# A fused attention, Fourier mixing and feed-forward kernel on one core: another order of all steps, and fifteen dummy matmul steps instead of sixteen

## The chip, the core and the metric

The kernel runs on one core of a Trainium2 chip. The core has a matrix engine (PE, whose weight loads are listed as PEld), a vector engine (DVE), a scalar engine (ACT), a general engine (POOL), a sync engine that only issues transfers here (SP), and sixteen DMA engines. Each engine works through its own instruction stream in order. The metric is the device time of one execution in microseconds (us), less is better. Times below come from four unprofiled runs and from one profiled execution.

## What is computed

Eight batches, eight heads, 576 rows, 64 columns a head. First a linear attention with exponential features, then a real two-dimensional Fourier transform added to the result, a normalisation, and a feed-forward block:

```python
proj = x @ w_phi;  proj -= max(abs(proj))
phi(x) = concat[exp(proj), exp(-proj)]            # 256 features
kv = phi(k)^T v;   z = sum(phi(k))
attn = (phi(q) kv) / (phi(q) z + 1e-6)            # per head, 576 x 64
x = attn with heads side by side                  # 576 x 512
u = x + real(fft(fft(x, axis=1), axis=2))
un = (u - mean(u)) / sqrt(var(u) + 1e-6)
out = u + relu(un @ w_ch1) @ w_ch2                # 512 -> 2048 -> 512
```

## The kernel before, in words

Nothing schedules this kernel at run time. The work of the eight batches is cut into some 1,240 steps, each a stretch of Python between two `yield`s that issues a few instructions on several engines. The string `PLAN` (from line 23) has one letter for each step, and the loop at the end issues the steps in that order (`step`, called over `PLAN`). So the order of the letters is the order of the instructions in every engine's stream, and in the transfer queues of POOL and SP as well. An instruction still waits for its operands and for a free buffer; while it waits, all that stands behind it on its engine waits too.

A letter names a stream, and the n-th use of a letter is the stream's n-th step. In the texts, "T1.0" is step 0 of stream T for batch 1.

- G and J (batch 0 only): transposes of keys and queries on PE (`turn_part`, L368), copied out by ACT (L373) or DVE (L375). J0.2 is the tile of the last 64 rows of the queries.
- T (`steps`): projections of keys (L477, L491; batch 0 L790, L804) and queries (L597; batch 0 L665, L697) on PE with the exponentials on ACT. T1.0 is `keys4` of batch 1, whose exponentials are L482 and L483.
- P (`maxima`): query projections whose absolute maximum DVE takes (L555; batch 0 L755, L772 in `widest4`, and `turn_m` L730 to L740). R (`kmax`): the same for keys (L511; batch 0 L838). S (`scaled`): POOL scales the values (L451, L466; batch 0 L852, L869).
- M (`mixing`): eight steps of key-value products (L887), the combination of the heads (L987, then L994 to L1002; six steps in batch 0, eight later), then the transform along the rows. For batches 1 to 7 that is M.16 (the matmul `pm`, L1021, and L1025 on DVE), M.17 (`again(1)`, L1034), M.18 (`along_rows`, L1045, with SS), M.19 (L1065 and `again(0)`), M.20 (L1045 with CS, and `px`) and M.21 to M.25 (`pu`, L1104). In batch 0 the same steps are M0.14 to M0.18 and on. D (`folded`): four DVE steps of sums and differences, L903 to L927; batch 0 copies a row on ACT in between (L916, L917).
- N and U: normalisation, its transpose (DMA, or PE in batch 0, L1159) and its scales. F (`forward`): 68 steps a batch of feed-forward: 32 of `hidden` (L1219 on PE, L1223 on ACT) and the rest of `output` (L1230 and L1277 on PE, L1236 on DVE).
- K, V, Q: loads of keys, values and queries of a later batch, issued by POOL (L284). B and A: their DMA transposes, issued by SP (L408, L410; L420 to L422). W: the loads of the two feed-forward weights (L93, L95), 2 MB each, by POOL. C, H, Z: constants, sines (L238 to L249, H0.0 to H0.3 are on ACT) and padding.
- Y (`stir`, L1325 to L1333): the dummy steps. Each issues four matmuls of 512 columns on a tile of ones into a PSUM tile that nobody reads (L1330). They use the PSUM pool `pk`, which has one buffer.

PSUM tiles come from three pools: `pj` (two buffers), `pk` (one) and `pb` (three). The order was written by a search outside the kernel; neither its costs nor its due times are in the file.

Of the kernel before, what the change touches and what calls it, by code (L numbers as in the profile page):

```python
# [20 lines left out]


PLAN = (
    "YYCCYCYGCGZTGRTGZTZTZRZJQQGSTJRKTPYTSTPRYTWJJJRMPTMTSSMTPPSTPTMTZQMTMMTMPMMVKBTCMTMDTYMVHMYYDYYDDAHM"
    "HYYHTHMMMHKMTTRMNMTMYQNNYVMSNTKNMFFNFNRRFSTPFTPTUFWMNFFMNFFSFRTFVMFFTCURPSYUBNTUTFSUFMFQKTFMFTPPMQTP"
    "VMTFFPUTFUMTMFFAFMMTFFMQFMFDFRFMFTVFFFFRFMFTFFMFFPFFTFFFQDDFFFRFMFTKFFDMTFFFFTFMFFMFRTFMRTFMFSSSSTTM"
    "NPFFTNPBTMMMSMQFTMTPPMFFMFFTMFFFPVTAMFFFPNFFMTFFMNNKUMFFVMMFFQTMFFTFRMRFFTFFFQFMFFMFMFFFPTFFRFFFFDFD"
    "VFTPFFFDFFDKTPRFTFFMMTSFFBFFFMMSSFFMFFRTMTMFFTNMSMFFFTNPPMFMTFFFTMTFSTPMFFFMFFQPFTFMFFVFNMFFFMKTFFAM"
    "NNMFFMFUMFVFFMVQFFMFTTRFFMFFFKFRFFMTQFFFDTMRFFFFFDTPFFFTDDFRPFFFFFMTFTFMFFMFBMRFSSMFFTTTMFMTFFFTFNFN"
    "SFMTTMMFFFPMFTMSTPPMFFSMTFFMNFPFMFFPFFVKMNQKFFMNMUFFMFFMFFVMFAFMFQMFFMFTTRFQRFFFTVFMFFFFDFTPFRFFFPDT"  # L30
    "FFFTFFFDFFFDRTMTMFFFFMBFSMFFSMRFTFTTMSFMFTFNMMMTMFTFFFMNFPSSTMTNFFFFTPPMFFFMFTFPQMFVFKFPFFMFFMANMFFN"
    "FFMKFFMFTUTFMFFRFRFFSVFMFFFFFTMFTFQFRMFDVTFFFMTRFFDFFFFFFFDFFDFTMFTBQFMFFMSFMFRFMFTFTTMFFSMTNFTNFFMP"
    "SMFFMMTFMPTFSMTFFMTPFMFTFFQMFNPPPFVMFFAMFFPFNNUMVFMFTFMFMFFFMFRFFMTRTFSFFFFFPFFMFVFMTFFRFFTFDFDFPTFF"
    "FFDDFRFFTTMMFFFFFFMMFRSFTFFMTFTMTFFNTFSMNFFFMTFTTFMFMFMTSPFMFFFFMFFSMFTPPMFFFMFFMNPFMFFPNNFUMMFFFFMF"
    "FMFFFMMFFFFFFMFFMFFFDFFDFFFDFFDFMFFFFMMFMFMFFFMNMFNFFFFFFFFMMFFFFFFFFFFFFFFFFFFFFNMNFNFFFFFUFFFFFFFF"
    "FFFFFFFFFFFFFFFFFFFFFFFFFFFFFFFFFFFFFFF"
)


# [1 line left out]
def kernel(  # L41
# [11 lines left out]
    B, H, S, D = q.shape  # L53
    DF = w_phi.shape[1]
    C = H * D
# [1268 lines left out]
        return run  # L1324

    def stir(b):
        for i in range(16):
            ps = pk.tile([128, 512], F32, tag="pk", name="idle")
            for x in range(4):
                nc.tensor.matmul(  # L1330
                    ps[:], lhsT=ones_b[:], rhs=ones_b[:].unsqueeze(1).to_broadcast([128, 4, 128]),
                    start=True, stop=True,
                )  # L1333
            yield

    def fold_later(b):
# [4 lines left out]
        "U": (scales, 1), "P": (part(0), 7), "T": (part(1), 18), "R": (part(2), 5),  # L1341
        "S": (part(3), 5), "K": (fetch_k, 2), "V": (fetch_v, 3), "Q": (fetch_q, 3),
        "A": (arrive, 1), "B": (arrive_k, 1), "W": (load_ffn_weights, 2),
        "C": (constants, 6), "H": (sines, 6), "Y": (stir, 16), "G": (turn_first_k, 5), "J": (turn_first_q, 5), "Z": (pads, 6),
    }
    LONGER = {("N", 0): 10, ("U", 0): 7, ("M", 0): 24, ("T", 0): 20}
    at_ = {name: (1 if name in "KVBQA" else 0, 0) for name in STREAMS}
# [51 lines left out]
```

## Time and profile before

| | us |
|---|---|
| median of 4 runs (lowest, highest) | 429.33 (427.49, 430.65) |
| the profiled execution's own time | 428.03 |
| its span, first to last instruction | 426.3 |
| PE busy | 403.3 |
| DVE busy | 331.0 |
| ACT busy | 311.6 |
| POOL busy | 207.7 |
| dummy matmuls, 64 of L1330, busy | 19.1 |
| feed-forward matmuls L1219, L1230, L1277, busy | 141.7, 125.0, 14.9 |

The span is shorter than the time by 1.7 us, which lies before the first and after the last instruction. Busy matmuls overlap (one is started before the last has drained), so the sum of single durations is more than busy time. The granted PE clock is 1.00 in nearly the whole run; its mean is 0.994.

### The profile page before, as it was taken

The numbers are of one execution on the slowest core, as the hardware profiler recorded it, in microseconds if no ns is written. First come the engines' busy times: TensorE is split into PE (matmuls) and PEld (weight loads), VectorE is DVE, ScalarE is ACT, GpSimd is POOL, SyncE is SP. The second block draws the span as 40 slices with busy tenths as digits, with TensorE's granted clock in tenths as the row PEclk, the third lists the DMA queues.
The fourth block names the chain that finished last, engine by engine and source line by source line (L and its number), as shares of the span: only waits on it lengthen the run. The fifth ranks groups of instructions, "written<-read, shape, count | busy, mean of one in ns | idle before, by whom it ended". The sixth has DMA issues, their size and how long they took to land.

```text
span 426.3 us, 10494 instructions
## 1 busy us (share of the span) xinstructions
PE 403.3 (95%) x4126; PEld 255.6 (60%) x4126; DVE 331.0 (78%) x682; ACT 311.6 (73%) x690; POOL 207.7 (49%) x271
## 2 busy tenths in 40 slices
PE   8789789997999999999999999999999999999994
PEld 3465466643766558554775558565866567657562
DVE  5889787899789985998879885998899868965302
ACT  7986999747975799488947998688958796455450
POOL 7992578532964291826573273935554333300100
PEclk9899999999999999999999999999999999999999
DMA  8999879994698946994499269695472141104204
GB/s 219 176 185 162 116 91 168 146 139 86 116 133 85 115 80 93 120 110 84 83 160 121 52 80 132 85 115 104 78 97 49 27 87 32 27 1 79 68 23 86
DMA packets 108700, 42.70 MB, mean 100 GB/s; under 512 B 82859, under 2 KB 103595, under 8 KB 108651
## 3 DMA queue, kind: packets, MB, share of 16 engines
q0 software_dynamic: 45936, 16.60, 37.3%
q1 hardware_dynamic: 62479, 25.31, 33.7%
q8 instruction: 32, 0.52, 0.5%
q10 hardware_dynamic: 236, 0.13, 0.1%
q14 instruction: 17, 0.14, 0.1%
HBM read 36.77 MB, written 9.44 MB: 108 GB/s over the span
## 4 chain that ended last, share of the span: by engine, by line
PE 46%; DVE 32%; ACT 15%; issue 2%; POOL 2%; DMA 1%; DVEq 0%; ACTq 0%; POOLq 0%
PE psf L1219 16%; PE pso L1230 13%; DVE cb L999 5%; DVE R L903 4%; DVE MK L511 4%; DVE tg L994 4%; PE kv L887 3%; ACT HT L1223 2%; PE pso L1277 2%; DVE CEO L1034 2%; DVE MQ L555 2%; PE pu L1104 2%; DVE rd L1001 2%; DVE X L1236 2%; PE psD L1045 2%
## 5 line engine op out<-in xcount | busy, mean ns | idle before, releaser
L1219 PE MATMUL psf<-UT,W1b 128*128 128x320 bf16 (+1 forms) x1024 | 141.7, 286 | 1.5 <-ACT HT L1223 0.7
L1223 ACT ACTIVATE HT<-psf 128x256 bf16<-128x256 f32 (+1 forms) x256 | 100.8, 425 | 34.0 <-PE psf L1219 26.4
L1230 PE MATMUL pso<-W2b,HT 128*128 128x512 bf16 x512 | 125.0, 379 | 0.0
L1219 PEld LDWEIGHTS <-W1b 128*128 128x128 bf16 x1024 | 94.4, 98 | 29.8 <-issue 3.6
L1230 PEld LDWEIGHTS <-HT 128*128 128x128 bf16 x512 | 46.0, 98 | 44.8 <-issue 1.4
L1002 POOL TENSOR_TENSOR X<-cb,rd 128x320 f32<-128x320 f32 x56 | 41.5, 745 | 39.0 <-DVE rd L1001 36.1
L466 POOL TENSOR_TENSOR VCn<-VS,VCn 128x512 bf16<-128x512 bf16 x28 | 29.7, 1059 | 41.9 <-ACT VCn L461 33.5
L555 DVE TENSOR_REDUCE MQ<-psq 128x8 f32<-128x1024 f32 (+1 forms) x32 | 34.2, 1085 | 15.0 <-PE psq L547 14.7
L1236 DVE SCALAR_TENSOR_TENSOR X<-pso,rs,X 128x512 f32<-128x512 f32 x32 | 23.6, 736 | 22.0 <-PE pso L1230 21.9
L497 ACT ACTIVATE KPn<-psk 128x1024 bf16<-128x1024 f32 x28 | 28.6, 1020 | 14.7 <-DVE MK L511 14.5
L497 ACT ACTIVATE KPp<-psk 128x1024 bf16<-128x1024 f32 x28 | 28.8, 1027 | 11.1 <-PE psk L491 11.1
L451 POOL TENSOR_TENSOR V4N<-VS,V4N 64x256 bf16<-64x256 bf16 x14 | 8.8, 632 | 52.5 <-ACT V4N L447 47.7
L1094 DVE TENSOR_TENSOR X<-pu,X 128x512 f32<-128x512 f32 (+3 forms) x49 | 23.5, 529 | 14.0 <-PE pu L1104 13.8
L511 DVE TENSOR_REDUCE MK<-psk 128x8 f32<-128x1024 f32 x28 | 33.7, 1207 | 0.4 <-ACT KPn L497 0.3
L1190 POOL TENSOR_TENSOR rs<-VE,mhalf 128x5 f32<-128x5 f32 (+1 forms) x9 | 10.3, 1145 | 41.3 <-DVE VE L1189 41.2
L466 POOL TENSOR_TENSOR VCp<-VS,VCp 128x512 bf16<-128x512 bf16 x28 | 29.6, 1059 | 0.0
L606 ACT ACTIVATE QPHP<-psh 128x1024 bf16<-128x1024 f32 x28 | 29.1, 1039 | 0.5 <-PE psh L597 0.3
L606 ACT ACTIVATE QPHN<-psh 128x1024 bf16<-128x1024 f32 x28 | 29.3, 1045 | 0.0
L1150 ACT ACTIVATE UN<-X,MV 128x512 bf16<-128x512 f32 (+1 forms) x35 | 24.8, 724 | 5.4 <-issue 2.7
L1174 DVE BATCH_NORM_STATS2 st<-X 128x6 f32<-128x512 f32 (+1 forms) x40 | 27.0, 675 | 0.1
L284 POOL DMA_DIRECT2D QS<-in_q_dram x28 | 23.7, 849 | 4.0 <-DMA QT<-QS 4.0
L987 PEld LDWEIGHTS <-QPHP 128*128 128x128 bf16 x280 | 21.0, 98 | 4.5 <-DVE cb L999 0.5
(464 smaller groups left out, 800.6 us busy)
## 6 DMA issues: line engine op xcount, KB each, us to landing
out_dram<-X SPq DMA_DIRECT2D x16, 256.0 KB
out_dram<-X SPq DMA_DIRECT2D x64, 64.0 KB
QS<-in_q_dram POOLq DMA_DIRECT2D x14, 256.0 KB, 5.6
KS<-in_k_dram POOLq DMA_DIRECT2D x7, 512.0 KB, 6.9
VS<-in_v_dram POOLq DMA_DIRECT2D x14, 256.0 KB, 5.3
W1b<-in_moe_w_ch_dram POOLq DMA_DIRECT2D x1, 2048.0 KB, 13.9
W2b<-in_moe_w_ch_dram POOLq DMA_DIRECT2D x1, 2048.0 KB, 18.3
W2b<-in_k_dram SPq DMA_DIRECT2D x2, 512.0 KB
```

The lines of the kernel that those rows point to most:

```text
L466: nc.gpsimd.tensor_tensor(out=VC[:, hs, :, 0:D], in0=values[b][0][:, hs, :].rearrange("p h (j d) -> p h j d", d=D), in1=VC[:, hs, :, D:D + ...
L497: nc.scalar.activation(out=KP[:, hs, :, :].rearrange("p e (jp jj) f -> p jj (e jp) f", jj=2), in_=psk[:], func=AT.Exp, scale=sgn,)
L511: nc.vector.tensor_reduce(out=MK[:, 2 * pr:2 * pr + 2, :].rearrange("p e (jp jj) -> p jj (e jp)", jj=2), in_=tiles[pr][:], axis=AX.X, op=A ...
L555: nc.vector.tensor_reduce(out=o, in_=i[:], axis=AX.X, op=ALU.max, apply_absolute_value=True)
L606: nc.scalar.activation(out=o, in_=psh[:], func=AT.Exp, scale=sgn)
L1002: nc.gpsimd.tensor_tensor(out=X[:, :, D * h:D * h + D], in0=cb[:, :, 0:D], in1=rd[:].to_broadcast([128, 5, D]), op=ALU.mult,)
L1150: nc.scalar.activation(out=UN[0:M, c, :], in_=X[0:M, c, 0:C], func=AT.Identity, scale=-1.0, bias=mv[0:M, c, 0:1],)
L1174: nc.vector.bn_stats(out=st[0:M, :], in_=X[0:M, c, 0:C])
L1219: nc.tensor.matmul(ps[:], lhsT=W1b[:, cc, 128 * hh:128 * hh + 128], rhs=UT[:, cc, lo:hi], start=(cc == 0), stop=(cc == NCC - 1),)
L1223: nc.scalar.activation(out=HT[:, hh, lo:hi], in_=ps[:], func=AT.Relu, scale=-1.0)
L1230: nc.tensor.matmul(po[:], lhsT=HT[:, hh, at:at + 128], rhs=W2b[:, hh, :], start=(hh == 0), stop=(hh == NHH - 1),)
L1236: nc.vector.scalar_tensor_tensor(out=U[:, c, 0:C], in0=po[:], scalar=scale_of[b, c], in1=U[:, c, 0:C], op0=ALU.mult, op1=ALU.add,)
```

## The change

`PLAN` is replaced by another order of the same steps, and the dummy stream Y has 15 steps where it had 16. No other line differs: every other step is in both orders, once each.

```diff
 PLAN = (
-    "YYCCYCYGCGZTGRTGZTZTZRZJQQGSTJRKTPYTSTPRYTWJJJRMPTMTSSMTPPSTPTMTZQMTMMTMPMMVKBTCMTMDTYMVHMYYDYYDDAHM"
-    "HYYHTHMMMHKMTTRMNMTMYQNNYVMSNTKNMFFNFNRRFSTPFTPTUFWMNFFMNFFSFRTFVMFFTCURPSYUBNTUTFSUFMFQKTFMFTPPMQTP"
...
+    "YCYYCCYZZGCZGTTZGRZWGTTRTJGSTJRPTPSTYRTJRJPSTTMJMSSMPPZTTPMKQTMVMTMTMPMKMTTCQMMTBDQTHHYMMVKYAHHHHYYD"
+    "DYDMYTMMMMKTTVRMNWTMMYNTSNMNYNRRFFFNFSNUMTPTYPTFMFRTUFBFMSTFFFURCMUNSFNPMTTPPFSMQNUTFVMFFTFKMTQQTPM"
...
 )
...
     def stir(b):
-        for i in range(16):
+        for i in range(15):
             ps = pk.tile([128, 512], F32, tag="pk", name="idle")
...
-        "C": (constants, 6), "H": (sines, 6), "Y": (stir, 16), ...
+        "C": (constants, 6), "H": (sines, 6), "Y": (stir, 15), ...
```

Written out as steps, the parts of the two orders that the prediction speaks of are these.

| place | before | after |
|---|---|---|
| Y ahead of the first transpose G0.0 | 4 | 4 |
| Y from there to M0.0 | Y0.4, Y0.5 | Y0.4 |
| Y from M0.0 to T1.0 | 7 | 6 |
| Y from T1.0 to F0.0 | 2 | 2 |
| the last Y | Y0.15, after F0.13 | Y0.13 after F0.3, Y0.14 after F0.52 |
| QT4 and its maxima | J0.2 J0.3 J0.4 R0.4 M0.0 P0.2 | J0.2 R0.4 J0.3 P0.2 S0.2 T0.9 T0.10 M0.0 |
| first POOL transfers | Q1.0 Q1.1 before S0.0, K1.0 and W0.0 after it | W0.0 before S0.0; K1.0 Q1.0 after S0.4 |
| around the sines | H0.0 D0.1 H0.1 M0.14 H0.2 Y0.11 Y0.12 H0.3 T1.0 | H0.0 to H0.5, then D0.1 M0.14 Y0.10 T1.0 |
| second weight load W0.1 | after F0.5 | after N0.0, ahead of F0.0 |
| batch 2, rows | M2.16 M2.17, 5 F, M2.18 M2.19, 2 F, M2.20 | M2.16 P3.2, 6 F, M2.17 F M2.18 R3.3, 3 F, M2.19 F M2.20 |

From F0.0 on the rhythm of the two orders is alike: most steps stand within five F steps of where they stood, and the last 40 steps are feed-forward of batch 7 in both.

More of the change, by code (lines that the diff above doesn't have):

```diff
@@ L23 @@
 PLAN = (
-    "YYCCYCYGCGZTGRTGZTZTZRZJQQGSTJRKTPYTSTPRYTWJJJRMPTMTSSMTPPSTPTMTZQMTMMTMPMMVKBTCMTMDTYMVHMYYDYYDDAHM"
-    "HYYHTHMMMHKMTTRMNMTMYQNNYVMSNTKNMFFNFNRRFSTPFTPTUFWMNFFMNFFSFRTFVMFFTCURPSYUBNTUTFSUFMFQKTFMFTPPMQTP"
-    "VMTFFPUTFUMTMFFAFMMTFFMQFMFDFRFMFTVFFFFRFMFTFFMFFPFFTFFFQDDFFFRFMFTKFFDMTFFFFTFMFFMFRTFMRTFMFSSSSTTM"
-    "NPFFTNPBTMMMSMQFTMTPPMFFMFFTMFFFPVTAMFFFPNFFMTFFMNNKUMFFVMMFFQTMFFTFRMRFFTFFFQFMFFMFMFFFPTFFRFFFFDFD"
-    "VFTPFFFDFFDKTPRFTFFMMTSFFBFFFMMSSFFMFFRTMTMFFTNMSMFFFTNPPMFMTFFFTMTFSTPMFFFMFFQPFTFMFFVFNMFFFMKTFFAM"
@@ L29 @@
[L29 to L33, printed above, removed]
@@ L34 @@
-    "FFDDFRFFTTMMFFFFFFMMFRSFTFFMTFTMTFFNTFSMNFFFMTFTTFMFMFMTSPFMFFFFMFFSMFTPPMFFFMFFMNPFMFFPNNFUMMFFFFMF"
-    "FMFFFMMFFFFFFMFFMFFFDFFDFFFDFFDFMFFFFMMFMFMFFFMNMFNFFFFFFFFMMFFFFFFFFFFFFFFFFFFFFNMNFNFFFFFUFFFFFFFF"
-    "FFFFFFFFFFFFFFFFFFFFFFFFFFFFFFFFFFFFFFF"
+    "YCYYCCYZZGCZGTTZGRZWGTTRTJGSTJRPTPSTYRTJRJPSTTMJMSSMPPZTTPMKQTMVMTMTMPMKMTTCQMMTBDQTHHYMMVKYAHHHHYYD"
+    "DYDMYTMMMMKTTVRMNWTMMYNTSNMNYNRRFFFNFSNUMTPTYPTFMFRTUFBFMSTFFFURCMUNSFNPMTTPPFSMQNUTFVMFFTFFKMTQQTPM"
+    "FVFFPTMTAUFUFTFMMFFMFFMFKMFRQVTRTFFFFFFDMFFMFFPFDFTDFFRTTFFFFFFMFFDFYTFFTMRFFFFMFSMSFFRMFTFSTMTFNTMF"
@@ new lines @@
+    "NPMMMMTFMTFMBSTPMFFSQFFTFMFVFPPVTMFKFFNMPFFMFPTFQNNUMFFMAFMFFMFFMFFKMFTTFFRMFVFFRFFFTMFDFFTPFFFFFFDF"
+    "DRPFFFDMTPFFTFFFFMFMRFTFFSMTFMFSFRTTMNFFSFFFMTNFMFMSFTPPMMBFFQTMTPFFMTSQFFMFFMTFFVMFTFVPFQFFMTFFMNNN"
+    "UMFFAMFMFTMFFMFVRFFFMTFFFRFFKMTKFFFMFTFDFRFFFTFFFTFFDDFDRPFFMFFFFMQTTFMMRSFFFSFTSMSFTTTFMFFFFNTSFMNF"
+    "MBMTFFPMMTQVFQFTMTFFMPTFFVMKFNPPPFMFFMFFPNFFMNFFUMMFFKMFMFAFMFFMFMFQFTRVMFTFFFFFRMSFFTFDFPTRQFFFFFTP"
+    "FFFTDFFFDFRFFDMTFFFMTFMMSFFFRSQMFFTFMSTTTFFNMMSFFTMNFPMMFFTFTMTBFVFTMFFFTVMFFFNKPPPMFFFMFFMFFMFNFPNF"
@@ L37 @@
+    "UMFFAKMFFMFFMFFTTMFFRFFFVRMQFTFFFMTRFFMFFTDFFFTFFDFDFFDFFRTMFTFFFMFMSMFFFRSFTMFTFMTTSFNTFMNFFFFMMMTM"
+    "SVFFPTBFFTMPFFMPSQFVMFFMTNPPFQMFFPTMFFAFPFFMNNUMFMFFMFMFTFMFFPRFMFFFTFFFFVRFTDFFMFFTFMFFFFRFTFFTDFFD"
+    "DPFRFFTMTFFFFMFMSFFMSFRFTMFTFTMFTFNSTMNMFFMFMFTTMFTFFFTMFPFFFFSFMFFTFFMFSPPPFMFFMFFMNNFFPFFNFUMMFFMF"
+    "MFFFFMFFMFFMFFMFFMFFFFFFFDFDDFDFMFFFMFMFMFMFFMNMNFFFFFFFFMMFFFFFFFFFFFFFFFFFFFFNFFFNFFMFNFFFUFFFFFFF"
+    "FFFFFFFFFFFFFFFFFFFFFFFFFFFFFFFFFFFFFF"
 )
@@ L1343 @@
         "A": (arrive, 1), "B": (arrive_k, 1), "W": (load_ffn_weights, 2),
-        "C": (constants, 6), "H": (sines, 6), "Y": (stir, 16), "G": (turn_first_k, 5), "J": (turn_first_q, 5), "Z": (pads, 6),
+        "C": (constants, 6), "H": (sines, 6), "Y": (stir, 15), "G": (turn_first_k, 5), "J": (turn_first_q, 5), "Z": (pads, 6),
     }
```

## Prediction

> **What bounds the kernel now.** I read the page first, then busy time by stretches of 20 us, then the engines' timelines in the stretches that are not full, then the chain of waits.
>
> ```profile
> span 426.3 us, 10494 instructions
> PE 403.3 (95%) x4126; PEld 255.6 (60%) x4126; DVE 331.0 (78%) x682; ACT 311.6 (73%) x690; POOL 207.7 (49%) x271
> ```
>
> ```profile
> 0.00:20.00 20.00, 16.73 (x120) 8.69 (x121) 13.82 (x35) 16.50 (x29) 17.52 (x38) 0.91 1.02 210
> 20.00:40.00 20.00, 17.67 (x285) 11.84 (x285) 16.85 (x40) 14.53 (x32) 12.72 (x17) 1.00 1.01 160
> 40.00:60.00 20.00, 15.74 (x158) 9.91 (x158) 15.71 (x43) 18.55 (x40) 12.34 (x18) 1.00 0.82 113
> 100.00:360.00 260.00, 254.57 (x2717) 164.34 (x2717) 217.65 (x422) 207.12 (x470) 136.37 (x165) 1.00 0.71 93
> ```
>
> The columns after the stretch are busy us of PE, PEld, DVE, ACT and POOL, then the granted PE clock. From 100 to 360 us PE is busy for 254.57 of 260: PE is the bound there, and an order cannot take matmuls away. Before 60 us it is another kernel: PE is idle for 9.9 us of 60 though it is being fed dummies, and ACT, at 18.55 of 20, is the fullest engine from 40 to 60.
>
> Busy PE hides small gaps, because matmuls overlap. So I gave each matmul of the timeline the spacing that its form has when it runs back to back (109 ns for 256 columns, 216 ns for 512, as the chain's "411.09 6.91 PE pso L1230 x32" shows) and called the rest of the spacing a gap. Of 426.3 us, 373 are matmul issue, 14 of them dummies, and about 53 are gaps: 20 before 60 us, 26 between 60 and the last matmul, 7 after it. The last 7 follow the last matmul in both orders. An order can work only on the 20 and the 26.
>
> Two places carry the 20. The first is around 17 to 22 us, PE's timeline and then DVE's:
>
> ```profile
> 17.01 1.52 PE L1330 MATMUL idle<-ones_b 128*128 128x512 bf16 x4
> 18.46 0.46 PE L368 MATMUL pst<-ident,HT 64*128 64x64 f32 x4
> 20.70 0.29 PE L887 MATMUL kv<-VCp,KPp 128*128 128x65 bf16 x4 [0.76 <-POOL VCp L869]
> 21.10 0.41 PE L766 MATMUL psq<-wphi,QT 64*64 64x128 bf16 x8
> ```
>
> ```profile
> 18.32 2.35 DVE L838 TENSOR_REDUCE MK<-psk 128x8 f32<-128x1024 f32 x2
> 21.55 1.28 DVE L772 TENSOR_REDUCE MQ<-psq 64x4 f32<-64x512 f32 x2 [0.88 <-PE psq L766]
> ```
>
> A dummy step stands ahead of the transpose of the last query rows (18.46), and the product kv, which waits for POOL, ahead of the projection at 21.10. DVE idles 0.88 us for it, and this reduction is on the chain. The second place is around 40 us, ACT's timeline and then PE's:
>
> ```profile
> 39.18 0.41 ACT L916 CAST HI<-R 1x257 bf16<-1x257 f32 x1 [2.95 <-DVE R L912]
> 41.32 0.70 ACT L249 ACTIVATE CD<-ga,halfpi 128x512 bf16<-128x512 f32 x1
> 42.81 1.28 ACT L482 ACT_TABLE_LOAD   x1 [0.79 <-PE ps L477]
> ```
>
> ```profile
> 40.16 2.10 PE L1330 MATMUL idle<-ones_b 128*128 128x512 bf16 x8
> 42.32 0.41 PE L477 MATMUL ps<-wphi,KT 64*64 64x128 bf16 x8
> ```
>
> ACT idles 2.95 us with three sines still to do, does them after 39.8, then waits for the projection of T1.0, which sits behind two dummy steps, and only then loads its table. The chain runs through the dummies (40.32, 41.24), L477 and this load.
>
> **The change part by part.** All sums are against the profiled execution, 428.03 us; the median of four is 429.33, which is 1.3 us higher, and the forecast is put on the median.
>
> *Sixteen to fifteen dummy steps.* A step at full clock is 4 x 216 ns = 0.86 us of PE. The four ahead of the first transpose stay four, so nothing changes before 7 us from this. The step that goes is Y0.5, the 1.52 us at 17.01. It is worth what the chain behind it gains, counted next. The last dummy step stands inside a full PE in both orders (64.25 before, after F0.52 in the new one) and costs 0.86 us in both.
>
> *Maxima of the last query rows ahead of M0.0.* J0.2 no longer waits for a dummy, and P0.2 no longer stands behind kv. What DVE waits for ends earlier by up to 0.88 us, its idle time; next it has the reductions of R0.4, already there. POOL issues W0.0 (0.82) before S0.0 instead of two query loads (2.05), and neither K1.0 nor W0.0 among the scalings (0.72 + 0.82), so POOL's end of the scalings (28.47) comes about as much earlier and does not take the gain away. Gain 0 to 0.9; taken 0.9, since both engines on that chain are freed.
>
> *Sines and T1.0.* H0.0 to H0.3 are table load 1.28 and 1.00 + 1.09 + 0.61 + 0.70 on ACT, 4.7 us; from 33.9 they end at 38.6, inside the idle 2.95, ahead of HI at 39.18. The load at 42.81 then waits only for one dummy step instead of two, 1.03 us. What is late next is the row transform: ET is copied at 45.07, held by ACT until then though its matmuls were issued by 43.2. So the gain is between 0, if DVE's chain (43.04 to 44.36) holds DT as now, and 2.0, the whole earlier end of the table load. Taken 1.1, the dummy step and little more.
>
> Both gains come before 60 us, and what follows to 72 us is ACT work without a pause, so they pass on. Together 2.0.
>
> *Loads.* K1.1 is issued after Q1.0 and V1.0. With POOL free near 27.5 and 0.35 + 0.72 + 0.91 + 1.27 + 0.98 of issue, it is out at about 31.7, as now (31.49 + 0.98 ends at 32.5). Its median landing of 6.9 us has W1b's 13.9 us no longer ahead of it. Nothing is taken for it; if it is late, the transposes on SP (38.54) and T1.1 move with it, 0 to 1 us. W0.1, ahead of F0.0, lands 10 us earlier; 0.
>
> *Rows of the transform, batches 1 to 7.* The DVE chain from pm to the last CEO is 0.78 + 1.03 + 0.69 + 1.91 + 0.6 us, with its wait on pm about 5.9. The PE work that covers it (steps M.16 to M.20, counted by the spacings above) is before 6.6, 4.2, 3.8, 4.3, 4.3, 5.3, 3.9 us, and after 7.3, 6.7, 5.1, 4.2, 5.1, 5.2, 3.7. This is the cover that now fails in batch 2:
>
> ```profile
> 148.21 1.06 PE L1045 MATMUL psD<-CS,CEO 128*128 128x289 bf16 x6 [0.86 <-DVE CEO L1034]
> ```
>
> But the new order puts maxima of 1.13 us each in the middle of the chain: P3.2 and R3.3 in batch 2, R2.3 in batch 1. Cover grows by 1.3 in batch 3 and 0.8 in batch 5 (bound of the gain -2.1); the three maxima bound the loss at +3.4. Taken -0.5, nearest to batch 2's own 0.86, since 6.7 of cover against 5.9 + 2.3 leaves a shortage of 1.5 where it was 1.7.
>
> *All else* moves within about five feed-forward steps (2.2 us of PE). It can hit any of the 26 us of gaps; no row prices it. I take 0 and bound it by -2 and +3.
>
> Sum: -0.9 - 1.1 - 0.5 = -2.5, so 425.5 against the profiled execution, and 426.8 against the median.
>
> [...] The clock first:
>
> ```profile
> 12.00:14.00 2.00, 1.01 (x13) 0.70 (x14) 2.00 (x3) 1.90 (x6) 2.00 (x4) 1.00 0.97 302
> 16.00:18.00 2.00, 2.00 (x20) 1.21 (x20) 1.69 (x4) 1.98 (x5) 1.85 (x4) 0.50 1.79 179
> 22.00:24.00 2.00, 1.02 (x25) 0.73 (x21) 1.87 (x5) 2.00 (x6) 1.51 (x2) 1.00 0.94 135
> ```
>
> After a stretch half idle (12 to 14) the clock was 0.50 from 14.6 to 18.0; after a like stretch at 22 to 24 it stayed 1.00. So fewer dummies may or may not bring a second such stretch, and by rows it would cost at most half of its 3.4 us, 1.7; I take none, since PE is not the bound there. [...]
>
> **The rivals.** *The startup gains are swallowed* (no change): KT lands late or DVE's chain holds DT as before; then only -0.5 to 0 is left, 428.8 to 429.3. For it: ACT is 18.55 of 20 busy anyway. Against it: ACT has a plain 2.95 us hole. *Maxima in the transform's chain* (slower): if PE runs dry for the three added maxima, 3 x 1.13 = 3.4 us in batches 1 and 2, it gives 430.7 with the startup gain and 432.7 without. It decides where DVE's chain plus the maxima is longer than the cover: 8.2 against 6.7 in batch 2 (it will), 7.0 against 7.3 in batch 1 (just not); other batches of this size would take it beyond 1%. *The gaps at full PE shrink too* (faster): cover of batches 3 and 5 counts in full (-2.1) and the other moves give -2: 429.33 - 2.0 - 4.1 = 423.2. *The change does not do what it says*: the dummies before 7 us stay four; the step gone is a later one. It alters no number above.
>
> **How the numbers follow.** Forecast 426.8, own range 424.5 to 428.5, chance 0.45. Swallowed 0.17; slower by maxima or other moves 0.25; gaps shrink too 0.13. One per cent, about what a measurement here can tell, is 4.3 us: faster is below 425.0, slower above 433.6. Faster takes 0.10 of the forecast and 0.12 of the last case, 0.22; slower takes half of the third, 0.13; within 1% is 0.65. The range runs from 422.5 to 433.0, leaving out 0.04 below and 0.12 above.
>
> **What would show it.** After: DVE's wait before L772 gone; no ACT hole before L916 and the table load of L482 by about 41; the first psf earlier than 51.8; 60 matmuls of L1330, 0.86 us less PE issue; psD of batch 2 still waiting for CEO, of batches 3 and 5 less. Wrong it would be if the first 60 us are not shorter, if a second stretch at clock 0.50 appears, or if PE's gaps from 100 to 360 us grow by more than 2 us.

## The result, and the profile after

The changed kernel takes 430.32 us (median of 53 runs, 427.81 to 432.63), the kernel before 428.30 in the same jobs (79 runs, 426.72 to 431.23). The ratio is 1.0039, 95% interval [1.0029, 1.0050]: 1.7 us slower (2.0 by the medians), where 2.5 us less was forecast. It is within the 1% that was called no change, and well outside the measurement's error. The forecast had been put on a median of four runs, 429.33, one of which is the profiled execution; over the 79 runs the kernel before is 1.0 us faster than that.

The page's head after:

```profile
span 428.7 us, 10483 instructions
PE 406.4 (95%) x4122; PEld 257.7 (60%) x4122; DVE 329.8 (77%) x682; ACT 311.3 (73%) x690; POOL 209.0 (49%) x271
```

Span 428.7 against 426.3, and the profiled execution took 430.46 against 428.03: this pair differs by 2.4, a little more than the medians. PE is busy 3.1 us longer, with one dummy step less. Busy time by stretches shows where most of it lies (busy us of PE, PEld, DVE, ACT, POOL, then the granted clock):

```profile
0.00:20.00 20.00, 15.49 (x111) 8.29 (x112) 14.46 (x35) 16.01 (x28) 17.49 (x37) 0.88 0.93 224
20.00:40.00 20.00, 19.73 (x291) 13.82 (x290) 15.82 (x39) 16.38 (x32) 14.74 (x22) 0.86 1.02 132
40.00:60.00 20.00, 16.63 (x155) 9.86 (x154) 17.38 (x44) 16.86 (x38) 11.41 (x15) 0.91 1.28 180
100.00:360.00 260.00, 254.92 (x2685) 163.50 (x2684) 215.55 (x419) 206.71 (x470) 136.97 (x165) 1.00 0.71 94
```

The clock column was 0.91, 1.00, 1.00, 1.00 before. PE from 20 to 40 us is 19.73 of 20 busy, with 291 matmuls for 285: its matmuls take longer up to 25.4 us (the eight of L766 0.63 us where they took 0.41). From 100 to 360 us PE is as full as before, so a loss there must be looked for in single waits.

To find where the time goes, I added up, in each order, the back-to-back issue times of all matmuls but the dummies, and compared the times at which the two kernels had the same sum behind them. The lag of the changed kernel (minus: it is ahead):

| time in the kernel before, us | 27 | 50 | 98 | 113 | 145 | 211 | 253 | 264 | 285 | 369 | 390 |
|---|---|---|---|---|---|---|---|---|---|---|---|
| lag after, us | +1.1 | +0.7 | +1.6 | -0.8 | -0.1 | -1.0 | -0.1 | +0.8 | +1.8 | +1.2 | +2.4 |

It starts late (the half clock), catches up by 2.4 us around 105 (a wait of 1.61 us on QPHN before is 0.38 after), and is level with the old order at 253. The loss of the profiled execution then comes in three jumps: at 253 to 264 (F4.0), between 264 and 285, and at 369 to 380 (row transform of batch 7). In the second PE has no wait of over 0.33 us, and its cause stays open.

PE's own list of waits names the first and the last: in all it waits 1.9 us for the transfer UT and 1.9 for the copy HI on ACT, where it waited 0.6 and 0.4 before (none longer than 0.4). The longest of each, in PE's timeline after:

```profile
255.25 1.48 PE L1219 MATMUL psf<-UT,W1b 128*128 128x256 bf16 x12 [1.29 <-DMA UT<-UN]
376.74 0.38 PE L1021 MATMUL pm<-HI,ones_b 128*128 128x512 bf16 x1 [1.35 <-ACT HI L917]
```

And the first 60 us, which the prediction rested on. DVE's timeline after:

```profile
21.14 1.28 DVE L772 TENSOR_REDUCE MQ<-psq 64x4 f32<-64x512 f32 x2 [0.85 <-PE psq L766]
```

PE's timeline after, ahead of it:

```profile
16.99 1.89 PE L1330 MATMUL idle<-ones_b 128*128 128x512 bf16 x4
...
20.47 0.63 PE L766 MATMUL psq<-wphi,QT 64*64 64x128 bf16 x8
```

L772 starts 0.41 us earlier than before (21.55), not 0.9, and its wait is still there: ahead of it one dummy step now takes 1.89 us, and the projection of L766 0.63 where it took 0.41. By L740 the gain has turned into a loss (24.91 against 24.54). Windows of 2 us show the cause:

```profile
18.00:20.00 2.00, 2.00 (x10) 1.07 (x8) 1.98 (x2) 1.41 (x3) 2.00 (x3) 0.50 1.06 209
20.00:22.00 2.00, 2.00 (x19) 0.96 (x17) 1.15 (x3) 0.90 (x2) 1.48 (x2) 0.50 1.06 215
22.00:24.00 2.00, 2.00 (x26) 1.94 (x25) 1.14 (x5) 2.00 (x6) 0.00 (x0) 0.50 1.06 215
```

The clock was 0.50 from 15.2 to 25.4, 10.2 us, where the kernel before had 3.4 us of it (14.6 to 18.0). ACT's timeline around the sines:

```profile
38.70 0.70 ACT L249 ACTIVATE CD<-ga,halfpi 128x512 bf16<-128x512 f32 x1
40.09 0.41 ACT L916 CAST HI<-R 1x257 bf16<-1x257 f32 x1 [0.69 <-DVE R L912]
42.64 1.28 ACT L482 ACT_TABLE_LOAD   x1 [1.84 <-PE ps L477]
```

The sines do lie ahead of HI now and the hole of 2.95 us is 0.69. But R is ready 0.9 us later, and the table load is only 0.17 us earlier.

### The profile page after: what moved, and what is told of

Same layout as the page of the kernel before. It is cut to its first block, busy times and chain, and to the rows that moved or that the text cites. A ratio compares the mean times of both kernels' runs of the same rounds, so it can differ in the third digit from the quotient of the medians.

```text
span 428.7 us, 10483 instructions
## 1 busy us (share of the span) xinstructions
PE 406.4 (95%) x4122; PEld 257.7 (60%) x4122; DVE 329.8 (77%) x682; ACT 311.3 (73%) x690; POOL 209.0 (49%) x271
## 4 chain that ended last, share of the span: by engine, by line
PE 52%; DVE 31%; ACT 10%; DMA 3%; issue 2%; SPq 0%; POOL 0%; DVEq 0%
PE psf L1219 17%; PE pso L1230 14%; DVE cb L999 6%; DVE tg L994 5%; DVE R L903 4%; PE kv L887 3%; DVE MK L511 3%; PE psD L1045 2%; PE idle L1330 2%; DVE rd L1001 2%; DMA UT<-UN 2%; DVE X L1236 2%; DVE MQ L555 2%; PE pu L1104 2%; PE pso L1277 2%
## 5 line engine op out<-in xcount | busy, mean ns | idle before, releaser
L1230 PEld LDWEIGHTS <-HT 128*128 128x128 bf16 x512 | 45.9, 98 | 44.2 <-issue 1.9
```

The source lines that it names most:

```text
L1230: nc.tensor.matmul(po[:], lhsT=HT[:, hh, at:at + 128], rhs=W2b[:, hh, :], start=(hh == 0), stop=(hh == NHH - 1),)
```

## The experiments

In all of them the steps are the same; only their order, the number of dummies, or one store is changed. "Old" and "new" are the two orders. A kernel that goes from old to new at a step F takes the old order up to it, then the steps that are still to do in the new order. Ratios are to the kernel before, on the same chip. A ratio is worked out over the runs and is not the quotient of the two medians (they differ by up to 0.3% here); where a part is given a price in us, it is the ratio's.

### Which part of the order loses

**The start alone.**

```diff
-PLAN: old
+PLAN: new up to F0.0, then old; 14 dummy steps
```

> The new order up to the first feed-forward step F0.0 (13 dummy steps there), then the remaining steps in the old order (one more dummy). Theory A, the clock: the loss is in the first 60 us, where the new kernel ran 10.2 us at half clock after 15.2 us (before: 3.4 us) because a dummy step is gone; this kernel then has the whole loss, +1.5 to +2 us on before. Theory B, late waits: the start is worth at most the lag that the two traces show at 65 us of equal PE work, +0.6 us, so this kernel is within +0.6 us of before or even faster.

Measured: 428.69 us against 428.51, ratio 0.9988 [0.9968, 1.0007]. The start is not where the kernel loses; whether it gains, this does not tell.

**The middle alone.**

```diff
-PLAN: old
+PLAN: old to F0.0, new to F3.0, then old; 16 dummy steps
```

> The old order up to F0.0 and from F3.0 on, the new order between (batches 0 to 2 of the feed-forward); 16 dummy steps. Theory A: no change. Theory B: the traces' lag goes from +0.6 at 65 us to -1.0 at 210 us with one more full dummy in it, so this kernel is 1 to 1.5 us faster than before.

Measured: 430.08, ratio 1.0017 [0.9991, 1.0043]: not told from no change.

**The late part alone.**

```diff
-PLAN: old
+PLAN: old to F3.0, then new; 16 dummy steps
```

> The old order up to F3.0 (205 us), then the new order of what is left; all 16 dummies, early as before. Theory A: no change, within 0.3 us of before. Theory B: the waits of PE for UT in batch 4 (1.3 us at 254 us) and for the folded row in batch 7 (1.3 us at 375 us) come with the late part, so it has the whole loss and more: +2 to +3.4 us.

Measured: 433.23, ratio 1.0078 [1.0049, 1.0106], 3.3 us slower. The loss is here, more of it than the whole change has. The three parts add up to +3.5 us (-0.5, +0.7, +3.3), twice the whole: a spliced kernel also pays at the places where the orders meet (the last pair below shows it), so the parts give the place of a loss better than its size. The wait at F4.0 has grown to 2.19 us in this trace, and the clock was halved behind it (rows in the last section).

**Batches 0 and 1.**

```diff
-PLAN: old
+PLAN: new up to F1.30, then old; without the last dummy, 14 dummy steps
```

> The new order up to F1.30 (about 134 us), the old order behind it, and without the last dummy step, which the new order has in the middle of the feed-forward (14 dummies). Theory E: the start is worth -0.5 us, the gaps of 1.89 and 0.70 us of batch 1 go (-1.5 net), the dummy in a full PE goes (-0.86): 1 to 2.5 us faster than before. Theory F: within 0.5 us of before.

```diff
-PLAN: old
+PLAN: old to F0.0, new to F1.30, then old; 15 dummy steps
```

> The old order up to F0.0, the new one from there to F1.30, then the old one; 15 dummy steps, all ahead of F0.0. Theory E: the gaps of 1.89 and 0.70 us of batch 1 go and the dummy step among the first feed-forward steps too: 1 to 2 us faster than before. Theory F: within 0.5 us of before.

Measured: 427.41, ratio 0.9968 [0.9948, 0.9989], and 428.68, ratio 0.9994 [0.9969, 1.0019]. The new order for the first two batches and the old one behind it is faster than both kernels, by 1.4 us against the kernel before. It has 14 dummy steps, and it is the only one of 18 variants whose interval lies below 1, so the size may flatter it. Without the new start the gain cannot be told.

**The late part in three.**

```diff
-PLAN: old
+PLAN: old to F3.0, new to F4.5, then old
```

> The old order, with the steps from F3.0 to F4.5 in the new order, then old again. Theory A, the loss of the late part sits at the wait of F4.0 on UT: +1.0 to +3 us against the kernel before (the whole new late part gave +3.3), and the trace shows a wait of over 1 us ahead of F4.0. Theory B, the loss is spread over batches 4 to 7: +0 to +0.8.

```diff
-PLAN: old
+PLAN: old to F4.5, new to F6.0, then old
```

> The old order, with the steps from F4.5 to F6.0 in the new order, then old again. Theory A, the loss sits at F4.0 and at the folded row of batch 7: 0 to +0.5 us against the kernel before. Theory B, batches 4 and 5 lose on their own: +1 us or more.

```diff
-PLAN: old
+PLAN: old to F6.0, then new
```

> The old order up to F6.0, then the new order to the end, where the folded row of batch 7 stands six feed-forward steps later and its matmul pm waits for it. Theory A, this wait costs what the trace shows: +0.8 to +1.0 us against the kernel before. Theory B, it is made up for before the end, as going back to the old order there gave no net gain: 0 to +0.3.

Measured: 433.16, ratio 1.0074 [1.0048, 1.0100]; 429.21, ratio 1.0017 [0.9997, 1.0036]; 430.49, ratio 1.0022 [0.9998, 1.0046]. The stretch from F3.0 to F4.5 alone costs 3.2 us, as much as the whole late part. The other two cost at most 2 us each by their intervals, and cannot be told from nothing. In the trace of the first, all lag is in one place: +0.3 at 221, +0.7 at 253, +2.4 at 264, and the same +2.4 to the end. That execution took 430.38, and nine of the twelve runs took 432.56 to 434.40: what these lose beyond 2.4 us no trace shows.

**The old order put back in the changed kernel.**

```diff
-PLAN: new
+PLAN: new, with the old order from F3.10 to F4.5
```

> The changed kernel with the old order in one window only, from F3.10 to F4.5 (about 215 to 257 us), the new order on both sides. Theory E, single places: the changed kernel's extra gaps in this window are 0.86 us (M4.13 behind DVE's cb) and 1.42 instead of 0.52 us (F4.0 behind UT of batch 4), so it gains 1 to 1.8 us on the changed kernel: -0.1 to +0.9 us on before. Theory F, the loss is spread (clock or small gaps everywhere): within 0.5 us of the changed kernel, +1.2 to +2.2 us on before.

```diff
-PLAN: new
+PLAN: new up to F6.10, then old
```

> The changed kernel with the old order of all that is left from F6.10 on (about 355 us to the end). Theory E: the gap ahead of pm of batch 7 goes from 1.51 back to 0.54 us; 0.8 to 1.2 us faster than the changed kernel, +0.5 to +0.9 us on before. Theory F: within 0.5 us of the changed kernel.

Measured: 431.71, ratio 1.0070 [1.0040, 1.0100], and 429.90, ratio 1.0047 [1.0026, 1.0068]. Both take away their jump (none at 253 to 264, none at 369 to 380) and make another where the orders meet: +3.0 us at 211 to 221 in the first, +0.7 at 349 to 359 in the second. They settle nothing about size, and the first is slower than either theory allowed. So taking the stretch out of the changed kernel did not confirm the 3.2 us; in its own profile the lag grows by 0.9 us from 253 to 264, and by 1.9 to 285.

### The clock and the dummies

```diff
-PLAN: new
+PLAN: new, with one dummy step more, beside Y0.4; 16 dummy steps
```

> The new kernel with a sixteenth dummy step put back beside Y0.4, ahead of the reduction R0.3, at about 17 us, where the old order had two. Theory A: two dummy steps in the half-clock window give the clock back at 18 us as before, so the stretch of half clock is 3.4 us instead of 10.2 and the kernel is 1 to 2 us faster than the changed one, at or below before. Theory B: the clock comes back but the time stays within 0.5 us of the changed kernel, +1.2 to +2.2 us on before.

```diff
-PLAN: old, 16 dummy steps
+PLAN: old without Y0.5, 15 dummy steps
```

> The kernel before without its sixth dummy step (Y0.5, at 17.0 us), nothing else: the second half of the change alone. Theory A, the clock: one dummy less in the half-clock stretch keeps it longer at half, +0.5 to +2 us. The prediction's step: DVE's wait of 0.88 us for the last query rows goes, so -0.9 to 0. If neither, within 0.4 us of before: the dummy is worth nothing here.

```diff
-PLAN: new, 15 dummy steps
+PLAN: new without Y0.14 (after F0.52), 14 dummy steps
```

> The changed kernel without its last dummy step Y0.14, which stands after F0.52 between matmuls that follow each other without a gap. Theory A, PE's cover decides from there on: the 0.86 us of its four matmuls come off, 429.4 where the changed kernel has 430.3. Theory B, the dummy fills a gap or the time comes back at the next wait on the transfer UT: no change, 430.3. Theory C, the clock: with one dummy fewer another half-clock stretch comes, over 431.

Measured: 431.09, ratio 1.0046 [1.0023, 1.0069]; 429.33, ratio 0.9996 [0.9971, 1.0020]; 430.99, ratio 1.0032 [1.0005, 1.0059]. With the dummy back the clock was halved for 3.4 us again (15.8 to 19.2) and the time was not better. So the missing dummy step is not why the kernel is slower. What the late dummy in a full PE is worth these runs cannot tell: 0.86 us is inside their intervals, and so is nothing.

The third run's trace stands apart: its order is the changed kernel's up to F0.52, and its clock was full (1.00 in the rows of 0 to 20, 20 to 40 and 40 to 60 us). So it shows what the new start does when the clock doesn't halve. DVE's timeline in it:

```profile
19.89 1.27 DVE L772 TENSOR_REDUCE MQ<-psq 64x4 f32<-64x512 f32 x2
```

ACT's:

```profile
40.43 1.28 ACT L482 ACT_TABLE_LOAD   x1 [1.84 <-PE ps L477]
```

And PE's, at the start of the feed-forward of batch 0:

```profile
50.01 1.47 PE L1219 MATMUL psf<-UT,W1b 128*128 128x256 bf16 x12
```

L772 waits for nothing and starts 1.66 us earlier than before, the table load 2.38, and the first feed-forward matmul (51.79 before, 52.65 after) 1.78. The kernel with the late part alone begins with the old order. The mean clock of its trace, 0.992 over 431.7 us, stands for about 6.9 us at half clock; 3.4 of them lie at 257.6 to 261.0, and the other 3.5 are no more than what lies behind the last matmul in the profile after (3.9). So I take its first 60 us to be at full clock too. PE's timeline in it:

```profile
52.04 1.03 PE L1219 MATMUL psf<-UT,W1b 128*128 128x256 bf16 x8
```

So with the clock full on both sides the new start is 2.0 us ahead, as predicted. It seldom is: of the nine profiled executions that begin with the new order, that of the run without the late dummy has a mean clock of 0.996, and the other eight have 0.980 to 0.992. The first feed-forward matmul comes at 52.65 in the changed kernel (13.7 us at half clock ahead of it), at 53.6 with the start alone (mean clock 0.987) and at 52.10 with the dummy back (3.4 us from 15.8 on). With the old order it comes at 51.79 before (3.4 us from 14.6 on) and at 51.8 with the middle alone (mean clock 0.994). So in none of these three is the new start ahead.

At 253 us the execution without the late dummy is 2.1 us ahead of the kernel before, at 264 1.1, at 390 it is 0.6 behind: with a full clock at the start the late part loses 2.7 us, as the changed kernel's own profile loses 2.5 there.

How much the clock takes on average can be read from the mean clock of every run. In the profiles before and after the clock is 1.00 or 0.50 and nothing between, so (1 - clock) x span x 2 is taken as the time spent at half clock; 2.1 us of it before and 3.9 after lie behind the last matmul. In 70 runs of the kernel before (those beside all but the last two experiments) with less than 7.5 us of it the median is 428.06, in 54 with more 430.35; a straight line through all gives 1.1 us for each 3.4 us at half clock. The changed kernel has on average 2.1 us more of it than the kernel before, so 0.7 of its 1.7 us would be this (0.4 by the line through the changed kernel's own 54 runs, 0.6 us for each 3.4). It is not the main part: in runs with less than 7.5 us the changed kernel takes 430.13 against those 428.06.

### The store queue

SP issues the eight stores of output tile 1 (L1200, 5.1 us) ahead of the transposes of the next batch's UN. These kernels put those stores at the end of the batch, just ahead of the stores of its last tile (batches 0 to 6).

```diff
-            store(b, U, c)
+            if c != 1 or b == B - 1:
+                store(b, U, c)
...
+        store(b, U, 1)
```

> The kernel before, with the eight stores of the output tile c = 1 issued at the end of a batch's feed-forward instead of after its second output block (batches 0 to 6), so that SP issues the next batch's UT transposes ahead of them. Theory C, the store queue: SP spends 5.1 us on these stores ahead of the transposes, and PE waits for UT at the head of a batch; before has such gaps of 0.45 and 0.58 us (batches 3 and 4), so this gains 0.5 to 1 us. Theory D, the loss is in DVE's chains (folds and maxima): no change, within 0.3 us.

> The changed kernel with the same late stores. Theory C: its gaps ahead of the first hidden block are 0.83, 0.45 and 1.48 us in batches 2, 3 and 4, 2.7 us in all, so it gains 2 to 2.7 us on the changed kernel and comes to 0.4 to 1 us below before. Theory D: it stays at +1.2 to +2 us on before.

> The kernel with the old order up to F3.0 and the new one behind it, which was +3.3 us, with the late stores. Theory C: the wait of 2.3 us at batch 4 goes, and with it 2 to 2.5 us of the 3.3; +0.8 to +1.3 us on before. Theory D: +2.8 to +3.5 us.

Measured, in the order before, after, late part alone: 430.18, ratio 1.0016 [0.9991, 1.0041]; 435.76, ratio 1.0146 [1.0102, 1.0190]; 435.75, ratio 1.0146 [1.0103, 1.0188]. I had taken the stores for what holds UT. They are not, or not alone: F4.0 still waited 1.24 us in the second and 0.83 in the third (there the trace names DVE's X, L1285, as the last to come). In the second PE's waits for UT grew from 1.9 us in all to 4.9, in five places. The late stores cost the kernel before nothing that can be told, and the other two 3 to 5 us on top of their loss.

### The wait at F4.0

The last two runs put matmuls back ahead of F4.0, which the new order had moved behind it, in the isolated run (new order from F3.0 to F4.5 alone) and in the changed kernel. The edits are written out as steps.

```diff
-T5.16 M5.2 F4.0 F4.1 F4.2 T5.17 V6.1 M5.3 F4.3 F4.4 N4.2 P5.3 P5.4 M5.4
+T5.16 M5.2 P5.3 P5.4 M5.3 F4.0 F4.1 F4.2 T5.17 V6.1 F4.3 F4.4 N4.2 M5.4
```

> The run with the new order from F3.0 to F4.5 alone (433.2, +3.2 against the kernel before), with the key-value product M5.3 and the maxima P5.3 and P5.4 set ahead of F4.0, as the old order has them. Theory A, the loss is the wait of F4.0 on UT, and it comes of matmuls moved from ahead of F4.0 to behind it: the wait of 1.22 us falls to about 0.4 to 0.7, the time to 431 to 432.3. Theory B, the wait only shows a loss that sits elsewhere (a later start of UT, a busier POOL or ACT): the wait falls but the time stays at 433 or more.

```diff
-T5.16 M5.2 F4.0 F4.1 F4.2 T5.17 V6.1 M5.3 F4.3 F4.4 F4.5 N4.2 K7.0 P5.3 P5.4 P5.5 M5.4
+T5.16 M5.2 P5.3 P5.4 M5.3 F4.0 F4.1 F4.2 T5.17 V6.1 F4.3 F4.4 F4.5 N4.2 K7.0 P5.5 M5.4
```

> The changed kernel (430.3) with M5.3, P5.3 and P5.4 set ahead of F4.0, as the old order has them. Theory A, the wait of 1.29 us there falls to 0.4 to 0.7 and the time by as much: 429.4 to 429.9. Theory B, what is gained there is waited for again later: 430.3 or more.

Measured: 432.43, ratio 1.0081 [1.0052, 1.0111], and 430.73, ratio 1.0041 [1.0016, 1.0067]. The wait is gone, the time is not back. PE's timeline in the isolated run (F3.0 to F4.5 new):

```profile
255.98 1.48 PE L1219 MATMUL psf<-UT,W1b 128*128 128x256 bf16 x12 [1.22 <-DMA UT<-UN]
260.33 0.29 PE L887 MATMUL kv<-VCp,KPp 128*128 128x65 bf16 x4 [0.50 <-ACT kvh L895]
```

And in the same run with the matmuls put back:

```profile
256.24 0.29 PE L887 MATMUL kv<-VCp,KPp 128*128 128x65 bf16 x4 [0.68 <-ACT kvh L895]
260.73 0.29 PE L887 MATMUL kv<-VCp,KPp 128*128 128x65 bf16 x4 [1.18 <-ACT kvh L895]
```

With UT out of the way PE waits for ACT, twice, for as long together (1.86 us against 1.72). kvh is ACT's copy of the product kv, and UN, which UT is the transpose of, is ACT's as well. What holds UT in this run, though, is SP:

```profile
245.61 5.12 SPq L1200 DMA_DIRECT2D out_dram<-X  x8
250.83 3.32 SPq L1167 DMA_TRANSPOSE UT<-UN  x2
```

UN was ready at 249.92 and 251.44. SP was done with the stores at 250.73 and issued the two transposes one behind the other, from 250.83 to 254.15. Before, UN was ready at 248.29 and 251.22, and the transposes were issued at 250.19 and 251.52, behind stores that began 0.64 us earlier. So in the isolated run UN is ready only 0.8 us ahead of the end of the stores, and to take one of the two away leaves the other. The two transposes vary as well: with the late part alone the order is the same and they are issued from 250.85 on, but they took SP 3.72 us instead of 3.32, and F4.0 waited 2.19 us instead of 1.22.

For ACT, look at the window from 240 to 250 us. The columns are as above, ACT's the fourth after the length. Before:

```profile
240.00:250.00 10.00, 10.00 (x74) 5.47 (x73) 8.52 (x18) 9.49 (x23) 6.58 (x8) 1.00 0.45 80
```

In the isolated run:

```profile
240.00:250.00 10.00, 9.84 (x72) 5.42 (x72) 8.42 (x18) 7.92 (x18) 6.95 (x8) 1.00 0.24 32
```

ACT is full in the old order (9.49 of 10) and has 1.6 us less work done in the new one. Of that, 0.5 us had been done ahead of 240 (30.68 us of ACT work from 200 to 240, against 30.19), so ACT is 1.1 us behind at 250. ACT's timeline there, before:

```profile
240.90 0.65 ACT L1056 CAST ET<-psD 128x578 bf16<-128x578 f32 x1 [0.36 <-PE psD L1045]
...
242.95 0.65 ACT L1056 CAST DT<-psD 128x578 bf16<-128x578 f32 x1
```

In the isolated run:

```profile
240.70 1.02 ACT L497 ACTIVATE KPp<-psk 128x1024 bf16<-128x1024 f32 x1 [0.66 <-PE psk L491]
241.98 0.65 ACT L1056 CAST ET<-psD 128x578 bf16<-128x578 f32 x1 [0.25 <-PE psD L1045]
...
244.02 0.65 ACT L1056 CAST DT<-psD 128x578 bf16<-128x578 f32 x1 [1.01 <-PE psD L1045]
```

In brackets is ACT's idle time: 0.36 us before, 0.66 + 0.25 + 1.01 = 1.92 in the isolated run (0.66, 0.31 and 0.96 in the changed kernel). While the row transform of batch 4 makes ET and DT, ACT has something else to do in the old order: T5.7's exponentials, whose projection stands ahead of M4.17, and S5.0's scales. In the new order T5.6 stands one F step later, T5.7 four, behind M4.17, and S5.0 22 F steps earlier. ACT runs dry, and behind 246 it has no idle time of over 0.2 us until 255.9 in which to make it up. Its idle time grows by 1.56 us there, of which 1.1 are not work done earlier; PE's lag grows by 1.7 from 253 to 264.

The second wait for kvh has a nearer candidate. ACT's timeline in the run with the matmuls put back:

```profile
259.77 0.74 ACT L1150 ACTIVATE UN<-X,MV 128x512 bf16<-128x512 f32 x1
```

This third UN (step N4.2) stands right ahead of the kvh that PE then waits 1.18 us for. The old order has it ahead of F4.0, at 253.49. That ACT is the cause at all is read from the traces: no kernel that puts T5.7 and S5.0, or N4.2, back alone was run.

## Why the prediction was wrong

**The step that failed is "All else ... I take 0".** It had been bounded by +3 with no row to price it, and the late part alone costs +3.3 us, the stretch from F3.0 to F4.5 alone +3.2. In the changed kernel's own profile the part behind 253 us costs 2.5. I had treated the move of steps by "about five feed-forward steps" as a shift of PE's work, and costed PE's cover. The runs show the place. The traces suggest that such a shift matters where the other engine is full: ACT, 9.49 of 10 busy from 240 to 250 before, waited 1.92 us for PE in the isolated run instead of 0.36, and 10 us later PE waited for what ACT and SP had to deliver. How much of the 3.2 us this is stays open: the changed kernel has the same waits of ACT, and its lag grows by 0.9 at F4.0. The page's average for ACT, 73%, hides this. I used ACT's full stretch (18.55 of 20) for the first 60 us and looked for none behind.

**The folded row of batch 7** belongs to the same term. D7.0 stands six F steps later, so PE waits 1.35 us for HI where pm waited 0.37 for something else. The lag jumps there by 1.2 us after, by 0.8 in the run with the new order from F6.0 on. Its price by runs is +0.9, with an interval that reaches zero.

**Maxima of the last query rows, -0.9.** The mechanism was right, the size too small: at full clock L772 waits for nothing and is 1.66 us earlier (1.64 against the old order at full clock, 21.53). In the changed kernel's own profile it was -0.41, and +0.37 by L740.

**Sines and T1.0, -1.1.** In the profile after, -0.17 at the table load. I had written that DVE's chain could hold the row transform; it did: PE waited 1.12 us for CEO ahead of the product with CS, 0.74 before. At full clock both steps together gave -1.78 at the first feed-forward matmul, against a predicted -2.0, and -2.03 against the old order at full clock. By runs the start alone is worth -0.5 us, interval -1.4 to +0.3.

**Clock, taken at none.** This is the second step that failed, and with it went most of the startup gain: -2.0 forecast, -0.5 by runs. The prediction named a second half-clock stretch as what would show it wrong, and set it at most 1.7 us. In the profile after the clock was at 0.50 for 10.2 us at the start, where it had been for 3.4, and for 3.4 more at 45.9 to 49.3. Set against the run without the late dummy, the half clock cost this execution about 2.5 us: its lag at 50 us is +0.7, where the same order at full clock has -1.8. I had argued that PE is not the bound there; in the profile after it was (2.00 busy of 2.00 in each window from 18 to 24 us, at a clock of 0.50). By runs it is worth 0.4 to 0.7 of the difference between the kernels. The 1.7 us fell short because they allowed for 3.4 us more at half clock, and there were 10.2 more ahead of the last matmul (13.7 against 3.4).

**Rows of the transform, -0.5.** Right in size by the waits of the two profiles, though not in place; by runs the middle alone is +0.7, interval -0.4 to +1.8, which shows no gain. The waits before were 0.53 (batch 1) and 0.86 (batch 2) for the operands of psD. After, none of over 0.15 us is left in batches 1 to 7, and in batch 2 the maxima that were moved into the chain have their own wait instead:

```profile
140.27 0.41 PE L527 MATMUL psq<-wphi,QT 64*64 64x128 bf16 x8 [0.65 <-DVE MQ L555]
```

0.53 + 0.86 - 0.65 is 0.7 gained. The rival that these maxima cost 3.4 us fell: one wait of 0.65 is all that the trace shows of them.

**The dummies.** The step dropped has no effect by itself that its run can tell (ratio 0.9996, -1.2 to +0.9 us). The rival "the startup gains are swallowed" came true in the profiled execution, with the clock as the visible cause and not KT.

## What to carry to other kernels

When steps are reordered, cost the move on every engine that is full in that stretch, not on the bounding engine alone: look at windows of 10 us around each move, and ask what each engine does while a serial chain runs. Taking away the wait that a profile names is not the same as taking away its cause; if the next wait on the same engine's products is as long, look 10 us upstream for idle time on the engine that makes them. Compare profiles at the same clock: here the new start looks worthless or worth 2 us by whether the clock halved (the first feed-forward matmul at 52.65 or at 50.01, where the old order has 51.8 to 52.0). Where a long fixed order is replaced as a whole, splice the two by batch: here the new first two batches with the old rest beat both (427.41), if only by 0.3%.

## What the runs showed of the hardware

In the profile before the clock was at 0.50 for 3.4 us ahead of the last matmul (14.6 to 18.0), in the profile after for 10.2 us (15.2 to 25.4) and for 3.4 (45.9 to 49.3), and in the run with the dummy back for 3.4 (15.8 to 19.2, in its windows of 14 to 26 us). That differed between executions that begin with the same order: the changed kernel and the run without the late dummy have the same steps up to F0.52, and the second was at 1.00 in each row up to 60 us.

Ahead of the first of these stretches PE was busy 1.01 of 2 us from 12 to 14 before, and 1.10 after. It was as busy from 22 to 24 us before (1.02 of 2; rows in the prediction), and the clock stayed at 1.00. In the profile after the clock was at 0.50 while PE was busy 2.00 of 2.00 in each window from 18 to 24 us (rows in the first section; 2.8 us of these six were f32 transposes, L368). What makes the clock halve or return these rows do not show.

In the run with the late part alone a wait of 2.19 us in the middle of the run was followed by a clock of 0.50. Its windows around F4.0:

```profile
256.00:258.00 2.00, 1.05 (x8) 0.89 (x9) 0.37 (x2) 0.38 (x1) 0.00 (x0) 0.90 1.04 149
258.00:260.00 2.00, 2.00 (x19) 1.58 (x17) 0.00 (x0) 1.26 (x3) 0.00 (x0) 0.50 1.06 215
```

PE had waited until 256.95, and the clock was at 0.50 from 257.6 to 261.0. The lag between 253 and 264 grew by about 3.3 us in that execution, by about 1.6 in the isolated run, where the wait was 1.22 us and the clock 1.00 in each window from 252 to 264.
